# Probabilities and gate values handled two tiles at a time in an attention and gated feed-forward kernel

## The chip, the cores and the metric

The kernel runs on one core of one Trainium2 chip. Its time is the device time of one launch in microseconds, the median of three runs: 981.09 us (981.05 to 982.55). The core has a matrix engine (TensorE, PE in the profile), a vector engine (VectorE, DVE), an activation engine (ScalarE, ACT), a general engine (GpSimd, POOL) and a queue engine (SyncE, SP) that issues nearly all transfers. Each engine works through its own list of instructions strictly in the order in which the built program holds them; an instruction that waits for a semaphore holds back everything behind it in its list.

## The reference

```python
# attention: 4 batches x 8 heads, 768 positions, 64 channels
scores = scale * q @ k.T
mask = window of blocks | first/last block row and column | sampled blocks   # 24 x 24 blocks of 32
scores = where(mask, scores, -1e9); scores -= max(scores, axis=-1)
attn = exp(scores); attn = attn / (sum(attn, axis=-1) + 1e-9)
x = attn @ v                                   # (4*768) x 512 after the heads are joined
# feed-forward: 512 -> 2048 -> 512; weights come as float64
h = x @ w_in
g = h              where h >= 1
    0              where h <= -1
    (h + 1)**2 / 4 between
out = g @ w_out                                # float32
```

## The kernel before, in words

The 32 heads (4 batches of 8) are worked through one after the other. Beside the heads of batch b+1 runs the feed-forward part of batch b; the feed-forward part of the last batch runs alone at the end. Matrix products are made of two-part numbers: a value is split into a rounded high part and the rest, both in a format that TensorE streams at full speed (fp32r), and two or three products are summed in PSUM.

**A head** has 768 columns of queries, worked in two halves of 384 (`HALF`), and six key tiles of 128. First come 12 products for the row maxima (`max_mm`, L267), each followed by a maximum on VectorE (`max_red`, L272); their result goes into extra rows of the query operand, so that the scores come out already shifted. Then for each half and each key tile `c`: two score products (`scores`, L318 and L319), the exponential on ScalarE (`expo`, L323) from PSUM into a tile `pt`, the rounded high part on ScalarE (`p_hi`, in the helper at L196, tile `ph`), the rest on VectorE (`p_lo`, L331, tile `pl`), a running sum over key tiles on GpSimd (`p_sum`, L338, tile `acc`) and two products with the values (`values`, L350 and L351). At the end of a half, ScalarE copies one part of the result out of PSUM (`o_tmp`, L355, tile `otmp`), VectorE adds the other (`o_add`, L360), and `acc_sum` (L373) folds GpSimd's sum into `psum` on VectorE.

**Whole heads.** For the pairs of heads listed in `WHOLE` (before: 0 to 4, so heads 0 to 9) the probabilities are not split. The value product takes them as plain float32 (L348), and a column of ones beside the values gives the sums, so `p_hi`, `p_lo`, `p_sum`, `o_tmp`, `o_add` and `acc_sum` fall away.

**The feed-forward part** goes in 8 half batches of 384 rows, each over 16 blocks `fi` of 128 hidden units. For a block: 12 products into the PSUM tile `hp` (`l1`, L472 to L474), of which there is one buffer, so that the next block's products wait until this block's gate is finished; then the gate: `g_relu` and `g_sq` on ScalarE (L478, L481), `g_max` on VectorE (L484), which is the last to read `hp`; then the high part `gh` on ScalarE (`g_hi`, L196), the rest `gl` on VectorE (`g_lo`, L493), and 9 products of 512 columns (`l2`, L500 to L502; L500 and L501 read `gh`, L502 reads `gl`).

**Weights** come as float64 pairs of words. `convert` loads 512 KB into a buffer `raw`, makes float32 with four VectorE instructions of 512 columns (L169 to L174) and splits them (L196, L180). The first weight matrix is converted during the heads of batch 0, the second during the first half batch of the feed-forward part (beside heads 8 to 11), from where it goes to DRAM and is loaded again for later half batches.

**The order** is made in two steps. Every piece of work gets a due time (`at(t, fn)`), in units of one key tile; a head has 12 units (`PER`), a block `fi` has 3. Tables such as `P`, `PA` and `PW` hold the offsets (`'lag'` is the distance from the scores of a key tile to its value products, `'l2'` the one from `l1` to `l2`). The pieces are then issued by due time to a scheduler, which sets each engine's list by when operands and buffers come free in its own reckoning. The lists in the built program can thus differ from the due times. Pools with 2 or 3 buffers (`pp`, `mt`, `cv`) limit how far work can run ahead.

Of the kernel before, what the change touches and what calls it, by code (L numbers as in the profile page):

```python
# [21 lines left out]
HALF = 384  # L22
# [15 lines left out]
def body(ctx, tc, qk_t, v, sampled_blocks, moe_w_in, moe_w_out, ind, cm, negd, ident, fold, out):  # L38
# [7 lines left out]
    pp = pool("pp", 3)  # L46
# [40 lines left out]
    def consts():  # L87
# [69 lines left out]
    def convert(t, src, dst, done=None):  # L157
        st = {}

        def load():  # L160
            st["raw"] = cv.tile([128, 512, 2], I32, name="raw", bufs=3)
            Q_RAW.dma_start(out=st["raw"], in_=src.bitcast(I32).rearrange("p (c w) -> p c w", w=2))
# [35 lines left out]
    def head(i, n0, b, h, pst):  # L198
# [122 lines left out]
        def expo(c):  # L321
            p = st["p", c] = pp.tile([128, HALF], F32, name=("pt", "ph", "pl")[c % 3] if wide else "pt")
            nc.scalar.activation(out=p, in_=st.pop(("ps", c))[:, 0:HALF], func=AF.Exp, scale=SCALE)  # L323

        def p_hi(c):
            ph = st["ph", c] = pp.tile([128, HALF], F32R, name="ph")
            rounded(nc.vector if c in (PH1 if i < 2 * H else PH2) else nc.scalar, ph, st["p", c])

        def p_lo(c):
            pl = st["pl", c] = pp.tile([128, HALF], F32R, name="pl")  # L330
            (nc.gpsimd if i < 2 * H and c in PL1 else nc.vector).tensor_tensor(out=pl, in0=st["p", c], in1=f(st["ph", c]), op=ALU.subtract)  # L331

        def p_sum(hf, c):
            if c == 1:
                st["acc", hf] = ac.tile([128, HALF], F32, name="acc")
            if c:
                prev = st["p", 0] if c == 1 else st["acc", hf]
                nc.gpsimd.tensor_tensor(out=st["acc", hf], in0=prev, in1=st["p", c], op=ALU.add)  # L338
# [110 lines left out]
    def moe(t0, p, b, hf, first):  # L449
# [26 lines left out]
        def g_relu(fi):  # L476
            r = g["r", fi] = mt.tile([128, HALF], F32, name="r")
# [9 lines left out]
        def g_hi(fi):  # L487
            gh = g["gh", fi] = mt.tile([128, HALF], F32R, name="gh", bufs=3)
            rounded(nc.scalar, gh, g["r", fi])

        def g_lo(fi):
# [29 lines left out]
        for fi in range(NF):  # L521
# [14 lines left out]
            for t in range(3):  # L536
                at(u + G["l2"] * p + t * p * G["l3"], l2, fi, t)
# [106 lines left out]
```

## Time and profile before

| | |
|---|---|
| median of 3 runs | 981.09 us (981.05 to 982.55) |
| profiled execution, whole | 980.94 us |
| its span | 979.0 us |
| PE busy | 945.3 us, 97% |
| DVE busy | 736.8 us, 75% |
| ACT busy | 646.3 us, 66% |
| POOL busy | 251.5 us, 26% |
| mean granted TensorE clock | 0.995 |

Busy time is not throughput on TensorE: successive products overlap in the records. A 384-column product is drawn 0.34 us long, but the next one starts 0.17 to 0.18 us later. What matters is therefore the distance between the starts of neighbours in the list, and where it is longer than that. On VectorE and ScalarE neighbours overlap by about a tenth of a microsecond when the second does not need the first. A row of the timeline reads: start in us, length in us, engine, source line, operation, output tile <- input tiles, shape, count; at the end, in brackets, an idle time before it and what ended it.

### The profile page before, as it was taken

To read this page: it belongs to the slowest core of one execution; us is meant where nothing else is said; L and a number is where in the kernel's file an instruction comes from. 1 tells how busy PE (TensorE), PEld (TensorE's weight loads), DVE (VectorE), ACT (ScalarE), POOL (GpSimd) and SP (SyncE) were. 2 spreads that over 40 slices of the span, in tenths; PEclk is the share of its full clock that TensorE was granted. 3 is DMA by queue.
4 is the path that set the end of the run, shared out by engine and by line. 5 is a ranking of instruction groups with operands and counts; after the bars stand their busy time and mean duration, and the time that the engine had idled before them with its cause. 6 is when DMAs were issued, how large, how long until landed. Compare 5 with 4: busy or idle time off the path is not lost.

```text
span 979.0 us, 14671 instructions
## 1 busy us (share of the span) xinstructions
PE 945.3 (97%) x4746; PEld 833.3 (85%) x4746; DVE 736.8 (75%) x1390; ACT 646.3 (66%) x1326; POOL 251.5 (26%) x229
## 2 busy tenths in 40 slices
PE   5898999999899999999999999999999999999998
PEld 3676677888789999998999899999999999899997
DVE  5897988779998888988888888888788885422222
ACT  4686787677677676767677667776767676433433
POOL 1000000013334443433434343433434343000000
PEclk9899999999999999999999999999999999999999
DMA  6756766754364544545556453646445442433442
GB/s 193 227 155 183 200 201 214 259 173 140 129 205 144 146 148 136 178 135 154 158 154 189 118 153 120 198 138 176 137 143 178 126 114 89 154 129 129 161 129 97
DMA packets 56216, 154.44 MB, mean 158 GB/s; under 512 B 9612, under 2 KB 17952, under 8 KB 56140
## 3 DMA queue, kind: packets, MB, share of 16 engines
q1 hardware_dynamic: 56100, 153.48, 52.0%
q8 instruction: 38, 0.62, 0.3%
q14 instruction: 38, 0.31, 0.1%
q10 hardware_dynamic: 40, 0.03, 0.0%
HBM read 100.92 MB, written 14.81 MB: 118 GB/s over the span
## 4 chain that ended last, share of the span: by engine, by line
PE 88%; DVE 5%; ACT 3%; DMA 2%; issue 2%; SPq 0%; ACTq 0%; DVEq 0%
PE oa L500 8%; PE oa L502 8%; PE oa L501 8%; PE hp L472 8%; PE hp L474 8%; PE hp L473 8%; PE pa L267 7%; PE pa L318 5%; PE pa L319 5%; PE po L350 5%; PE po L348 5%; PE po L351 4%; PE oa L348 3%; DVE mc L272 1%; PE oa L318 1%
## 5 line engine op out<-in xcount | busy, mean ns | idle before, releaser
L338 POOL TENSOR_TENSOR acc<-acc,pt 128x384 f32<-128x384 f32 x176 | 202.2, 1149 | 226.2 <-ACT pt L323 190.3
L272 DVE TENSOR_REDUCE mc<-pa 128x1 f32<-128x384 f32 x384 | 202.8, 548 | 24.1 <-PE pa L267 21.0
L196 ACT CAST ph<-pt 128x384 fp32r<-128x384 f32 x264 | 135.7, 514 | 88.2 <-PE po L350 84.5
L331 DVE TENSOR_TENSOR pl<-pt,ph 128x384 fp32r<-128x384 f32 x264 | 166.3, 630 | 35.6 <-ACT ph L196 34.9
L323 ACT ACTIVATE pt<-pa 128x384 f32<-128x384 f32 x288 | 140.6, 489 | 50.8 <-PE pa L319 42.0
L472 PE MATMUL hp<-x,wi 128*128 128x384 f32 x448 | 155.0, 346 | 2.9 <-DVE r L484 2.9
L500 PE MATMUL oa<-w,gh 128*128 128x512 f32 x384 | 153.6, 400 | 0.3 <-ACT gh L196 0.3
L502 PE MATMUL oa<-w,gl 128*128 128x512 f32 x384 | 151.4, 394 | 0.0
L473 PE MATMUL hp<-x,wi 128*128 128x384 f32 x448 | 151.4, 338 | 0.0
L474 PE MATMUL hp<-x,wi 128*128 128x384 f32 x448 | 151.2, 338 | 0.0
L501 PE MATMUL oa<-w,gh 128*128 128x512 f32 x384 | 150.8, 393 | 0.0
L267 PE MATMUL pa<-KA,QA 88*128 88x384 f32 x384 | 138.8, 381 | 5.3 <-DMA QA<-qkh 3.0
L338 POOL TENSOR_TENSOR acc<-pt 128x384 f32<-128x384 f32 x44 | 45.8, 1040 | 349.4 <-ACT pt L323 349.4
L484 DVE SCALAR_TENSOR_TENSOR r<-r,hp 128x384 f32<-128x384 f32 x112 | 61.7, 551 | 74.0 <-ACT r L481 73.6
L493 DVE TENSOR_TENSOR gl<-r,gh 128x384 fp32r<-128x384 f32 x128 | 83.7, 654 | 23.4 <-ACT gh L196 22.9
L478 ACT ACTIVATE r<-hp,half_c 128x384 f32<-128x384 f32 x112 | 65.1, 582 | 53.4 <-PE hp L474 50.3
L318 PE MATMUL pa<-QA,KA 102*128 102x384 f32 x288 | 99.3, 345 | 0.8 <-ACT pt L323 0.4
L319 PE MATMUL pa<-QB,KB 128*128 128x384 f32 x288 | 97.9, 340 | 0.0
L267 PEld LDWEIGHTS pa<-KA,QA 88*128 88x128 f32 x384 | 73.2, 192 | 27.8 <-DVE mc L272 6.7
L350 PE MATMUL po<-ph,vn 128*128 128x384 f32 x264 | 91.5, 347 | 2.3 <-DVE xun L360 1.9
L472 PEld LDWEIGHTS hp<-x,wi 128*128 128x128 f32 x448 | 84.5, 189 | 8.6 <-DVE r L484 4.2
L351 PE MATMUL po<-pl,vn 128*128 128x384 f32 x264 | 88.6, 336 | 0.0
(100 smaller groups left out, 1634.1 us busy)
## 6 DMA issues: line engine op xcount, KB each, us to landing
w<-wo_dram SPq DMA_DIRECT2D x112, 512.0 KB
qk<-in_qk_t_dram SPq DMA_DIRECT2D x32, 384.0 KB
raw<-in_moe_w_in_dram SPq DMA_DIRECT2D x16, 512.0 KB
raw<-in_moe_w_out_dram SPq DMA_DIRECT2D x16, 512.0 KB
wo_dram<-w SPq DMA_DIRECT2D x16, 512.0 KB
lv<-in_v_dram SPq DMA_DIRECT2D x32, 192.0 KB
KA<-qkh SPq DMA_DIRECT2D x32, 192.0 KB
QA<-qkh SPq DMA_DIRECT2D x32, 192.0 KB
```

Source lines behind the costliest of these rows:

```text
L267: nc.tensor.matmul(out=pm[:, 0:HALF], lhsT=QAi[0:KM, t * 128:(t + 1) * 128], rhs=KAi[0:KM, kh * HALF:(kh + 1) * HALF], start=True, stop=True)
L272: nc.vector.reduce_max(out=st["mc"][:, t, kh:kh + 1], in_=st.pop(("pm", t, kh))[:, 0:HALF], axis=AX.X)
L318: nc.tensor.matmul(out=ps[:, 0:HALF], lhsT=KAi[0:KA, ks], rhs=QAi[0:KA, cs], start=True, stop=False)
L319: nc.tensor.matmul(out=ps[:, 0:HALF], lhsT=st["KB"][:, ks], rhs=st["QB"][:, cs], start=False, stop=True)
L331: (nc.gpsimd if i < 2 * H and c in PL1 else nc.vector).tensor_tensor(out=pl, in0=st["p", c], in1=f(st["ph", c]), op=ALU.subtract)
L338: nc.gpsimd.tensor_tensor(out=st["acc", hf], in0=prev, in1=st["p", c], op=ALU.add)
L472: nc.tensor.matmul(out=hv, lhsT=wi[:, j, 0, fs], rhs=x[:, 0], start=(j == 0), stop=False)
L473: nc.tensor.matmul(out=hv, lhsT=wi[:, j, 0, fs], rhs=x[:, 1], start=False, stop=False)
L474: nc.tensor.matmul(out=hv, lhsT=wi[:, j, 1, fs], rhs=x[:, 0], start=False, stop=(j == NP - 1))
L500: nc.tensor.matmul(out=o, lhsT=gh[:, ts], rhs=w[:, 0], start=(fi == 0), stop=False)
L501: nc.tensor.matmul(out=o, lhsT=gh[:, ts], rhs=w[:, 1], start=False, stop=False)
L502: nc.tensor.matmul(out=o, lhsT=gl[:, ts], rhs=w[:, 0], start=False, stop=(fi == NF - 1))
```

## The change

Five things change together.

- The exponentials of two neighbouring key tiles go into one tile `[128, 2, 384]`. `p_hi` and `p_lo` then work on a pair: one instruction of 768 columns in place of two of 384. `p_sum` adds pairs: per half two additions of 768 and one of 384 that folds the two halves of the sum, in place of five of 384.
- In the feed-forward part `g_relu`, `g_sq` and `g_max` stay per block, but `g_hi` and `g_lo` work on two blocks at once. Both blocks' `l2` products thus depend on the gate of the second one. Due times of `l2` move: by 0.6 of a block for even `fi`, by 0.2 for odd ones.
- The float64 buffers `raw` go from 3 to 2; `ph` and `pl` have 2 pairs in place of 3 single tiles, `pt` 3 pairs, `gh` and `gl` 2 pairs in place of 3 singles.
- `WHOLE` loses its last pair: heads 8 and 9, the first of batch 1, are now split like all later ones.
- The value products of split heads get the distance `LAG = 4.0` in place of 3.5, and the feed-forward parts start half a unit later (`DELAY`).

```diff
-        ef = f(cv.tile([128, 512, 2], I32, name="raw", bufs=3)...
+        ef = f(cv.tile([128, 512, 2], I32, name="raw", bufs=2)...
...
         def expo(c):
-            p = st["p", c] = pp.tile([128, HALF], F32, name=("pt", "ph", "pl")[c % 3] if wide else "pt")
+            cp, k = divmod(c, 2)
+            if k == 0:
+                st["pp", cp] = pp.tile([128, 2, HALF], F32, name=("pt", "ph", "pl")[cp] if wide else "pt",
+                                         bufs=2 if wide and cp else 3)
+            p = st["p", c] = st["pp", cp][:, k]
...
+        def p_hi(cp):
+            ph = st["php", cp] = pp.tile([128, 2, HALF], F32R, name="ph")
+            rounded(nc.scalar, ph, st["pp", cp])
+        def p_lo(cp):
+            pl = pp.tile([128, 2, HALF], F32R, name="pl")
+            nc.vector.tensor_tensor(out=pl, in0=st["pp", cp], in1=f(st["php", cp]), op=ALU.subtract)
+        def p_sum(hf, cp):
+            if cp == 0:
+                return
+            if cp == 1:
+                st["acc2", hf] = ac.tile([128, 2, HALF], F32, name="acc")
+            acc = st["acc2", hf]
+            nc.gpsimd.tensor_tensor(out=acc, in0=st["pp", 0] if cp == 1 else acc, in1=st["pp", cp], op=ALU.add)
+            if cp == 2:
+                nc.gpsimd.tensor_tensor(out=acc[:, 0], in0=acc[:, 0], in1=acc[:, 1], op=ALU.add)
...
-                if not whole:
-                    at(s + G["ph"], p_hi, c)
-                    at(s + G["pl"], p_lo, c)
-                    at(s + G["ps"], p_sum, hf, c)
-                at(s + G["lag"], values, hf, c)
+                if not whole and c % 2:
+                    at(s + G["ph"] - 0.5, p_hi, c // 2)
+                    at(s + G["pl"] - 0.5, p_lo, c // 2)
+                    at(s + G["ps"], p_sum, hf, c // 2)
+                at(s + (G["lag"] if whole else LAG), values, hf, c)
...
+        def g_hi(fp):
+            gh = g["ghp", fp] = mt.tile([128, 2, HALF], F32R, name="gh")
+            rounded(nc.scalar, gh, g["rr", fp])
+        def g_lo(fp):
+            gl = mt.tile([128, 2, HALF], F32R, name="gl")
+            nc.vector.tensor_tensor(out=gl, in0=g["rr", fp], in1=f(g["ghp", fp]), op=ALU.subtract)
...
-            at(m + G["gh"], g_hi, fi)
-            at(m + G["gl"], g_lo, fi)
+            if fi % 2:
+                at(m + G["gh"], g_hi, fi // 2)
+                at(m + G["gl"] + 0.1, g_lo, fi // 2)
+            w = u + G["l2"] * p + (0.6 * p if fi % 2 == 0 else 0.2 * p)
             for t in range(3):
-                at(u + G["l2"] * p + t * p * G["l3"], l2, fi, t)
+                at(w + t * p * G["l3"], l2, fi, t)
...
-WHOLE = (0, 1, 2, 3, 4)
+WHOLE = (0, 1, 2, 3)
+LAG = 4.0
-DELAY = 3.672
+DELAY = 4.172
```

Three places in the engines' lists show what the scheduler makes of it. They lie in the steady part, at head 22 and at the feed-forward blocks that stand 57th and 58th of the 128 (counted from 0; called 57 and 58 below, an odd and an even one).

The first place is ScalarE's list around the gate of block 57: the exponential (`pt`), the gate's two steps (`r`), the copy `otmp` and the rounding `gh`. Before:

```order
L478 ACTIVATE r<-hp,half_c 128x384
L323 ACTIVATE pt<-pa 128x384
L481 ACTIVATE r<-r 128x384
L196 CAST ph<-pt 128x384
L355 COPY otmp<-po 64x384
L196 CAST gh<-r 128x384
```

And now:

```order
L327 ACTIVATE pt<-pa 128x384
L490 ACTIVATE r<-hp,half_c 128x384
L493 ACTIVATE r<-r 128x384
L365 COPY otmp<-po 64x384
L327 ACTIVATE pt<-pa 128x384 x2
L196 CAST gh<-r 128x768
```

Between the square (the last `r<-r`) and `gh` stood `ph` and `otmp`; now `otmp` and two exponentials stand there, and `gh` is 768 wide.

The second place is TensorE's list after the last `l1` product of block 57 (`hp<-x,wi`), up to the products that read its `gh` and `gl`. Before, 41 rows lie between the first and the last row shown:

```order
L474 MATMUL hp<-x,wi 128x384
L267 MATMUL pa<-KA_116,QA_114 128x384
L318 MATMUL pa<-QA_113,KA_115 128x384
L319 MATMUL pa<-QB,KB 128x384
...
L500 MATMUL oa_6170<-w,gh 128x512
L501 MATMUL oa_6170<-w,gh 128x512
L502 MATMUL oa_6170<-w,gl 128x512
```

And now, up to the products of block 56, which reads the first half of the same `gh`:

```order
L484 MATMUL hp<-x,wi 128x384
L267 MATMUL pa<-KA_116,QA_114 128x384 x2
L360 MATMUL po<-ph,vn 128x384
L361 MATMUL po<-pl,vn 128x384
L318 MATMUL pa<-QA_113,KA_115 128x384
L319 MATMUL pa<-QB,KB 128x384
...
L514 MATMUL oa_5783<-w,gh 128x512
L515 MATMUL oa_5783<-w,gh 128x512
L293 MATMUL pa<-idr,mr 6x128
L516 MATMUL oa_5783<-w,gl 128x512
```

Between the last `l1` product and the first reader of `gh` there are now 17 products of 384 columns: two for maxima, four for values, four for scores and seven of the next block's `l1` (in the lines left out). Before, the nine products that read block 56's gate stood in between as well. At the same place after block 59 there are 14, after blocks 61 and 63 there are 15 and 14 and one small product.

The third place is VectorE's list at the end of head 22, with `g_max` of block 58 (`r<-r,hp`), which frees `hp` for block 59. Before:

```order
L331 TENSOR_TENSOR pl<-pt,ph 128x384
L484 SCALAR_TENSOR_TENSOR r<-r,hp 128x384
L331 TENSOR_TENSOR pl<-pt,ph 128x384
L373 TENSOR_REDUCE psum<-acc 128x12
L493 TENSOR_TENSOR gl<-r,gh 128x384
```

And now:

```order
L506 TENSOR_TENSOR gl<-r,gh 128x768
L336 TENSOR_TENSOR pl<-pt,ph 128x768
L298 TENSOR_TENSOR QA_114<-pa,nd 6x768
L336 TENSOR_TENSOR pl<-pt,ph 128x768
L383 TENSOR_REDUCE psum<-acc 128x12
L496 SCALAR_TENSOR_TENSOR r<-r,hp 128x384
```

`g_max` stood ahead of the head's last `pl` and of `psum`, which waits for GpSimd's sum; now it stands behind both.

More of the change, by code (lines that the diff above doesn't have):

```diff
@@ L45, in body @@
     vp = pool("vp", 2)
-    pp = pool("pp", 3)
+    pp = pool("pp", 2)
     ac = pool("ac", 2)
@@ L160, in load @@
         def load():
-            st["raw"] = cv.tile([128, 512, 2], I32, name="raw", bufs=3)
+            st["raw"] = cv.tile([128, 512, 2], I32, name="raw", bufs=2)
             Q_RAW.dma_start(out=st["raw"], in_=src.bitcast(I32).rearrange("p (c w) -> p c w", w=2))
@@ L321, in expo @@
         def expo(c):
-            p = st["p", c] = pp.tile([128, HALF], F32, name=("pt", "ph", "pl")[c % 3] if wide else "pt")
[L323 to L338, printed above, removed]
+            cp, k = divmod(c, 2)
[3 more added lines that the diff above has]
+            p = st["p", c] = st["pp", cp][:, k]
+            nc.scalar.activation(out=p, in_=st.pop(("ps", c))[:, 0:HALF], func=AF.Exp, scale=SCALE)
+        def p_hi(cp):
+            ph = st["php", cp] = pp.tile([128, 2, HALF], F32R, name="ph")
+            rounded(nc.scalar, ph, st["pp", cp])
+            st["ph", 2 * cp], st["ph", 2 * cp + 1] = ph[:, 0], ph[:, 1]
+        def p_lo(cp):
+            pl = pp.tile([128, 2, HALF], F32R, name="pl")
+            nc.vector.tensor_tensor(out=pl, in0=st["pp", cp], in1=f(st["php", cp]), op=ALU.subtract)
+            st["pl", 2 * cp], st["pl", 2 * cp + 1] = pl[:, 0], pl[:, 1]
+        def p_sum(hf, cp):
[7 more added lines that the diff above has]
+                nc.gpsimd.tensor_tensor(out=acc[:, 0], in0=acc[:, 0], in1=acc[:, 1], op=ALU.add)
+                st["acc", hf] = acc[:, 0]
         def values(hf, c):
@@ L416, in head @@
                 at(s + G["ex"], expo, c)
-                if not whole:
-                    at(s + G["ph"], p_hi, c)
-                    at(s + G["pl"], p_lo, c)
-                    at(s + G["ps"], p_sum, hf, c)
-                at(s + G["lag"], values, hf, c)
+                if not whole and c % 2:
[3 more added lines that the diff above has]
+                at(s + (G["lag"] if whole else LAG), values, hf, c)
                 s += 1
-            u = s - 1 + G["lag"]
+            u = s - 1 + (G["lag"] if whole else LAG)
             if whole:
@@ L485, in g_max @@
                                            op0=ALU.min, op1=ALU.max)
[L487 to L491, printed above, removed]
-            gl = g["gl", fi] = mt.tile([128, HALF], F32R, name="gl", bufs=3)
-            (nc.gpsimd if first and fi % 4 in GL1 else nc.vector).tensor_tensor(out=gl, in0=g["r", fi], in1=f(g["gh", fi]), op=ALU.subtract)
+        def g_hi(fp):
+            gh = g["ghp", fp] = mt.tile([128, 2, HALF], F32R, name="gh")
+            rounded(nc.scalar, gh, g["rr", fp])
+            g["gh", 2 * fp], g["gh", 2 * fp + 1] = gh[:, 0], gh[:, 1]
+        def g_lo(fp):
+            gl = mt.tile([128, 2, HALF], F32R, name="gl")
+            nc.vector.tensor_tensor(out=gl, in0=g["rr", fp], in1=f(g["ghp", fp]), op=ALU.subtract)
+            g["gl", 2 * fp], g["gl", 2 * fp + 1] = gl[:, 0], gl[:, 1]
         def l2(fi, t):
```

12 lines of the change are left out of this document (7 added, 5 removed).

## The prediction

> **What bounds the kernel now.** I read the page first, then the busy time by stretch, then the idle time in front of the feed-forward products, and last the order in time of single instructions.
>
> ```profile
> PE 945.3 (97%) x4746; PEld 833.3 (85%) x4746; DVE 736.8 (75%) x1390; ACT 646.3 (66%) x1326; POOL 251.5 (26%) x229
> ...
> 195.80:293.70 97.90, 90.64 (x458) 78.16 (x457) 91.41 (x164) 70.31 (x148) 30.66 (x26) 1.00 0.50 162
> 293.70:832.20 538.50, 536.05 (x2821) 493.83 (x2820) 444.76 (x832) 382.81 (x800) 216.66 (x194) 1.00 0.50 147
> 832.20:979.00 146.80, 142.53 (x716) 128.06 (x714) 42.52 (x78) 59.60 (x112) 0.65 (x1) 1.00 0.39 133
> ...
> L500 PE MATMUL oa<-w,gh 128*128 128x512 f32 x384 | 153.6, 400 | 0.3 <-ACT gh L196 0.3
> L502 PE MATMUL oa<-w,gl 128*128 128x512 f32 x384 | 151.4, 394 | 0.0
> L472 PE MATMUL hp<-x,wi 128*128 128x384 f32 x448 | 155.0, 346 | 2.9 <-DVE r L484 2.9
> ```
>
> The three stretches (columns: length, then busy time of PE, weight load, DVE, ACT, POOL) are the heads 8 to 11 with the weight conversion, the heads 12 to 31, and the last batch's feed-forward part. In the second and third TensorE has no holes; its products stand in line. In the first VectorE is busy 91.41 of 97.90 us: there it is the bound, or nearly. The last three rows say the same from the other side: of all idle time in front of the feed-forward products only 0.3 us is a wait for `gh`, none for `gl`, and 2.9 us for the gate that frees `hp`. So over 685 us nothing gains time but work taken off TensorE, and everything that makes TensorE wait costs its full length.
>
> Why it does not wait today shows at one block (the odd block 57 of the order rows above):
>
> ```profile
> 573.65 0.34 PE L473 MATMUL hp<-x,wi 128*128 128x384 f32 x1
> 573.83 0.34 PE L474 MATMUL hp<-x,wi 128*128 128x384 f32 x1
> 581.30 0.39 PE L500 MATMUL oa<-w,gh 128*128 128x512 f32 x1
> 581.53 0.40 PE L501 MATMUL oa<-w,gh 128*128 128x512 f32 x1
> 574.21 0.58 ACT L478 ACTIVATE r<-hp,half_c 128x384 f32<-128x384 f32 x1 [0.32 <-PE hp L474]
> 574.80 0.49 ACT L323 ACTIVATE pt<-pa 128x384 f32<-128x384 f32 x1
> 575.18 0.52 ACT L481 ACTIVATE r<-r 128x384 f32<-128x384 f32 x1
> 576.38 0.48 ACT L355 COPY otmp<-po 64x384 f32<-64x384 f32 x1
> 576.76 0.51 ACT L196 CAST gh<-r 128x384 fp32r<-128x384 f32 x1
> 577.29 0.49 ACT L323 ACTIVATE pt<-pa 128x384 f32<-128x384 f32 x1
> 577.93 1.33 POOL L338 TENSOR_TENSOR acc<-acc,pt 128x384 f32<-128x384 f32 x1 [1.48 <-ACT pt L323]
> 578.29 1.38 DVE L493 TENSOR_TENSOR gl<-r,gh 128x384 fp32r<-128x384 f32 x1
> ```
>
> The last `l1` product starts at 573.83, `gh` is finished at 577.27 (576.76 + 0.51), `gl` at 579.67, and the first product that reads them starts at 581.30. Some 7.3 us of other products lie in between, against 5.7 us that the slower of the two takes. The rows also give TensorE's spacing: 0.175 us for 384 columns, 0.23 for 512.
>
> **The change, part by part.**
>
> *Heads 8 and 9 split.* A whole product and its split successor:
>
> ```profile
> 210.14 0.81 PE L348 MATMUL po<-pt,vn 128*128 128x384 f32 x2
> 210.96 0.34 PE L473 MATMUL hp<-x,wi 128*128 128x384 f32 x1
> 579.96 0.34 PE L350 MATMUL po<-ph,vn 128*128 128x384 f32 x1
> 580.14 0.34 PE L351 MATMUL po<-pl,vn 128*128 128x384 f32 x1
> 580.31 0.22 PE L293 MATMUL pa<-idr,mr 128*6 128x128 f32 x1
> ```
>
> From 210.14 to 210.96 lie the whole product and one L472 of 0.175 us, so it holds TensorE for 0.645 us; the two split ones take 0.35 (579.96 to 580.31). 24 of them: 24 x 0.295 = 7.1 us less on TensorE. But they lie in the stretch that VectorE bounds, and VectorE gets work.
>
> ```profile
> L228 DVE TENSOR_TENSOR qk<-qk,qkh 128x768 f32<-128x768 f32 x32 | 34.6, 1081 | 1.3 <-ACT qkh L196 1.2
> 579.68 0.54 DVE L331 TENSOR_TENSOR pl<-pt,ph 128x384 fp32r<-128x384 f32 x1
> 580.15 0.94 DVE L228 TENSOR_TENSOR qk<-qk,qkh 128x768 f32<-128x768 f32 x1
> 573.10 0.57 DVE L373 TRANSPOSE_TENSOR_REDUCE psum<-acc 128x12 f32<-128x384 f32 x1
> 569.85 0.83 ACT L196 CAST qkh<-qk 128x768 fp32r<-128x768 f32 x1 [0.63 <-DMA qk<-in_qk_t_dram]
> 570.59 0.48 ACT L323 ACTIVATE pt<-pa 128x384 f32<-128x384 f32 x1
> ```
>
> The trace has 768-column instructions of the same kinds: 0.94 us on VectorE when nothing hinders it (its mean of 1081 ns does hold hindrances), 0.83 on ScalarE. Neighbours are 0.47 apart on VectorE for 384 columns (579.68 to 580.15), that is 0.08 of overlap, so a 768 one takes 0.86 of the engine in place of 2 x 0.47 = 0.94: pairing saves 0.08 per pair, not half. On ScalarE it is 0.74 (569.85 to 570.59) in place of two times 0.41 (0.51 less the tenth of overlap), again 0.08. Heads 8 and 9 add on VectorE 12 pairs x 0.86 = 10.3 us, and four times an `o_add` (0.47) and an `acc_sum` (0.57 less the overlap) = 3.8; pairing gives back 20 x 0.08 = 1.6 there. 91.4 + 12.5 = 103.9 us no longer fit into 97.9. If VectorE is packed full, the stretch takes 6 us longer; if TensorE's saving comes through whole, 7 us less; if VectorE keeps the 93% it has now and the waits below come on top, some 21 more. I take **+6**, since VectorE stands at 93% already.
>
> *The gate by pairs of blocks.* This is the large term. Both blocks' products now wait for the second block's gate, and the order rows show 17, 14, 15 and 14 products of 384 columns between its last `l1` product and the first reader of `gh`, in four pairs that repeat every two heads. At 0.175 us that is 2.97, 2.45, 2.68 and 2.51 us of cover, where 7.3 stood. What the chain needs can be read at the end of the run, where nothing else runs:
>
> ```profile
> 969.97 0.34 PE L474 MATMUL pa<-x,wi 128*128 128x384 f32 x1
> 970.34 0.58 ACT L478 ACTIVATE r<-pa,half_c 128x384 f32<-128x384 f32 x1 [1.90 <-PE pa L474]
> 970.95 0.53 ACT L481 ACTIVATE r<-r 128x384 f32<-128x384 f32 x1
> 971.51 0.55 DVE L484 SCALAR_TENSOR_TENSOR r<-r,pa 128x384 f32<-128x384 f32 x1 [2.48 <-ACT r L481]
> 972.10 0.51 ACT L196 CAST gh<-r 128x384 fp32r<-128x384 f32 x1 [0.62 <-DVE r L484]
> 972.66 0.50 PE L500 MATMUL oa<-w,gh 128*128 128x512 f32 x1 [0.28 <-ACT gh L196]
> ```
>
> From the end of the last `l1` product's turn (969.97 + 0.175 = 970.14) it is 0.20 to the gate's first step, 0.81 to the square, 2.52 to the first reader. With `gh` at 0.83 in place of 0.51 that is 2.84 bare. In the steady part ScalarE's list now has `otmp` and two exponentials between square and `gh`. With neighbours a tenth apart in overlap (574.80 to 575.18 for an exponential of 0.49, 576.38 to 576.76 for `otmp`) the square holds the engine to 1.24, `otmp` to 1.62, the exponentials to 2.00 and 2.38, `gh` ends at 3.21 and TensorE can go on at 3.26. The gate's VectorE step is done by 1.92 and does not count. In two of the four pairs a copy of `vn` (0.51) stands in between too, which moves all by 0.29. Waits for `gh`: 0.29, 1.1, 0.58, 1.04.
>
> Then `gl`, 0.94 long, which TensorE wants 0.5 to 1.2 us after `gh` (two `gh` products and what stands between): at 3.49, 3.43, 3.55 and 3.69. Undisturbed it is there at 4.2 or 4.5, which makes the whole wait of a pair 0.7, 1.1, 0.65 and 1.05, on average 0.88. But it is not undisturbed. In the fence of block 57, `gl` took 1.38 us where 0.55 is its usual length: a GpSimd addition ran from 577.93 to 579.26, and `gl` ended 0.41 behind it. So VectorE's subtraction stands still until GpSimd's addition is through, and then needs its length less 0.14. Now GpSimd's first pair addition starts 0.1 to 0.15 us behind the first of the two exponentials (577.78 to 577.93 above), at 2.2 us on the same scale, a microsecond ahead of `gl`, and it is 768 wide.
>
> ```profile
> L338 POOL TENSOR_TENSOR acc<-pt 128x384 f32<-128x384 f32 x44 | 45.8, 1040 | 349.4 <-ACT pt L323 349.4
> L90 POOL MEMSET QA<- 64x768 f32 x2 | 1.4, 732 | 0.3 <-POOLq L624 0.3
> L91 POOL MEMSET vn<- 128x384 f32 x1 | 0.4, 427 | 0.1
> ```
>
> No 768 addition is in the trace. It takes at least the 1.02 of a 384 one and at most twice that; the memsets (427 ns for 384, 732 for 768) leave 0.12 fixed, which makes 0.12 + 2 x 0.90 = 1.92. I take 1.9, as the row nearest in kind scales that way. The addition then ends at 4.1 (4.4 with `vn`), `gl` at 4.9 (5.2), and the waits become 1.46, 1.8, 1.4, 1.55: on average 1.55 a pair. Heads 12 to 31 have 40 pairs: **+62**, with 35 if GpSimd does not hinder, and 13 for the bare chain (0, 0.4, 0.16 and 0.33 for `gh`; about 0.32 with `gl`). What ScalarE and VectorE have less to do meanwhile is worth nothing, since they wait for TensorE.
>
> The Trainium skill, SBUF — State Buffer, section "SBUF: two separate sides", says that a VectorE instruction with two SBUF inputs and a GpSimd one that reads SBUF take a port pair as an exclusive lock for the whole instruction. By that rule the 62 holds and not the 35; the row of 1.38 agrees.
>
> *The sum by pairs.* `acc_sum` now follows two additions of 1.9 and 1.02 behind the last exponential, and at every second head stands ahead of the `g_max` that frees `hp` (the third place of the order). Behind the last score product lie 0.2 + 0.49 + 0.1 + 1.9 + 1.02 + 0.57 + 0.55 = 4.8 us until `hp` is free; TensorE's list has 11 products of 384 and 9 of 512 columns there, 11 x 0.175 + 9 x 0.23 = 4.0. So 0.8 us at every second head, 10 times: **+8**. Where the last `pl` too stands behind GpSimd, it is up to 1.3 a head: 26. With a shorter addition: 0.
>
> *The last part.* After `l1` of an odd block 16 products lie ahead of `gh`'s reader, 2.73 us against 2.84 + 0.05, with `gl` 0.16 short: 15 pairs, 2.4 us. The last pair cannot be covered: before, 9 products of the last block but one (9 x 0.23 = 2.1) fill most of the 2.52, then none fill the 2.84; 2.4 us more. Together **+5**, between 2 and 6.
>
> *Two raw buffers, the wider distances.* Conversions are due 5.75 units apart, 12 us; 512 KB at the mean 158 GB/s of the page take 3.3. With two buffers a load starts one conversion earlier than its use, and hides. If VectorE is late the load is late by as much; 0, with 0 to 4. `LAG` and `DELAY` shift work on a full TensorE: 0.
>
> Sum: 979.0 + 6 + 62 + 8 + 5 = 1060 us of span. The profiled execution took 980.94, 1.9 beyond its span and 0.15 below the median, so **1062 us**.
>
> **The rivals.**
>
> *GpSimd does not hinder* (its wide addition is short, or `gl` gets ahead of it). For: GpSimd stands at 26%. Against: the row of 1.38. 979 + 6 + 35 + 8 + 5 + 2 = 1035.
>
> *Only the bare chain counts*, because the exponentials are through before the square. Against: their scores are in TensorE's list behind the last `l1` product. 979 + 0 + 13 + 0 + 5 + 2 = 999.
>
> *Faster: the saving on TensorE comes through.* The pairs' gates are finished in time, heads 8 and 9 shorten TensorE's list by 7.1 us, and VectorE, relieved of 0.08 a pair, does not hold the stretch back: 979 - 7 + 2 + 2 = 976. It decides if the wait is below 7.1 / 40 = 0.18 us a pair. For: TensorE is the bound and its list gets shorter. Against: even the bare chain is longer than three of the four covers.
>
> *Slower still*: the transfers that wait for a weight buffer sit in SP's one queue, and when TensorE is late those behind them are too; over 1096.
>
> **How the numbers follow.** The forecast, 1062, has 52%; GpSimd not hindering, 1035, 25%; the bare chain, about 999, 8%; faster, 976, 8%; no change 2%; slower still 5%. The low end is that second case with the first stretch at its best and no wait for sums, 979 - 7 + 35 + 0 + 2 + 2 = 1011, drawn to 1005 for part of the third; what it leaves out there is the rest of the third, no change and faster. The high end is 979 + 21 + 62 + 26 + 6 + 2 = 1096. Under 0.2% (2 us) no difference can be told here. Faster 8%, same 2%, slower 90%.
>
> **What would show it.** Right: idle time in front of L514 with the release by ACT `gh`, and of L516 with DVE `gl`, together near 60 us; PE busy falling well below 97% between the conversion and the last part; the row of `gl` 768 wide with a mean well above 0.94; GpSimd's 768 row near 1.9; a short wait of L482 for `g_max`; the last part 5 us longer. Wrong: `gl` at 0.94 on average (then 1035), GpSimd's wide addition near 1.0, or L514 and L516 with no idle time and the first stretch shorter (then 976). If the waits are there but TensorE's spacing closes up elsewhere, my premise that the list has no holes to give is wrong.

## The result and the profile after

The changed kernel takes 1124.83 us (median of 6 runs, 1123.4 to 1132.7) against 981.07 us before (6 runs): 1.148 times as long, 95% interval 1.144 to 1.151, or 144 us. The forecast was 1062, its range 1005 to 1096. The profiled execution took 1124.95 us, its span is 1123.1.

In the kernel before, the chain of work that ended last stood almost wholly on TensorE:

```profile
PE 88%; DVE 5%; ACT 3%; DMA 2%; issue 2%; SPq 0%; ACTq 0%; DVEq 0%
```

In the changed kernel, the head of the page and the groups that answer to those of the prediction (columns: busy time in us and mean of one in ns; then idle time in front and what ended it):

```profile
PE 998.5 (89%) x4750; PEld 830.2 (74%) x4750; DVE 795.2 (71%) x1218; ACT 619.3 (55%) x1138; POOL 259.1 (23%) x153
...
PE 49%; DVE 28%; ACT 11%; issue 5%; DMA 4%; POOL 4%; SPq 0%; POOLq 0%; ACTq 0%; DVEq 0%
...
L336 DVE TENSOR_TENSOR pl<-pt,ph 128x768 fp32r<-128x768 f32 x144 | 178.6, 1240 | 62.6 <-ACT ph L196 32.1
L345 POOL TENSOR_TENSOR acc<-pt 128x768 f32<-128x768 f32 x48 | 89.3, 1861 | 514.5 <-ACT pt L327 514.5
L345 POOL TENSOR_TENSOR acc<-acc,pt 128x768 f32<-128x768 f32 x48 | 92.1, 1918 | 185.8 <-ACT pt L327 185.8
L347 POOL TENSOR_TENSOR acc<-acc 128x384 f32<-128x384 f32 x48 | 74.2, 1546 | 3.8
L482 PE MATMUL hp<-x,wi 128*128 128x384 f32 x448 | 160.5, 358 | 39.4 <-DVE r L496 39.3
L516 PE MATMUL oa<-w,gl 128*128 128x512 f32 x384 | 152.3, 409 | 22.4 <-DVE gl L506 22.3
L514 PE MATMUL oa<-w,gh 128*128 128x512 f32 x384 | 157.5, 410 | 4.2 <-ACT gh L196 3.6
L267 PE MATMUL pa<-KA,QA 88*128 88x384 f32 x384 | 134.8, 388 | 28.3 <-DVE mc L272 17.6
...
L506 DVE TENSOR_TENSOR gl<-r,gh 128x768 fp32r<-128x768 f32 x64 | 75.3, 1176 | 20.8 <-ACT gh L196 20.8
```

TensorE fell from 97% to 89%, and the chain that ended last now leads over VectorE for 28% of the span (5% before). The two wide additions take 1.86 and 1.92 us on average (forecast 1.9) and `gl` 1.18 (0.94 when no addition runs as it starts). But the longest wait is not that for `gl`: it is that for `hp`, 39.3 us, and 17.6 more are waits for a bank that a maximum (`mc`) still reads.

From here on the span is cut where the turn of the last `l1` product of feed-forward blocks 0, 16 and 96 ends (0.175 us behind its start). The second piece, 16 blocks long, is the conversion stretch with about heads 8 to 11 (it begins earlier than the prediction's, which was cut at 195.8); the third, 80 blocks, holds about heads 12 to 31; the fourth is the last batch's feed-forward part. Busy time by stretch, before (columns: length, then busy time of PE, weight load, DVE, ACT, POOL, then granted TensorE clock, DMA share and GB/s):

```profile
163.00:284.80 121.80, 114.54 (x567) 97.36 (x567) 109.05 (x197) 85.95 (x176) 28.27 (x24) 1.00 0.56 182
284.80:841.00 556.20, 553.75 (x2913) 509.92 (x2913) 458.28 (x858) 393.50 (x821) 219.70 (x196) 1.00 0.51 148
841.00:979.00 138.00, 133.73 (x670) 120.17 (x668) 37.30 (x67) 56.14 (x105) 0.00 (x0) 1.00 0.40 134
```

and after:

```profile
163.70:308.80 145.10, 124.99 (x578) 105.66 (x578) 136.72 (x212) 90.64 (x165) 42.02 (x23) 0.92 0.49 160
308.80:978.00 669.20, 593.59 (x2905) 502.75 (x2904) 493.00 (x698) 366.25 (x663) 208.25 (x119) 1.00 0.42 122
978.00:1123.10 145.10, 138.84 (x679) 119.76 (x677) 35.77 (x52) 52.67 (x90) 0.00 (x0) 1.00 0.42 130
```

The 144 us are 23.3 in the conversion stretch, 113.0 in heads 12 to 31, 7.1 in the last part and 0.7 ahead of them. In heads 12 to 31 VectorE runs 160 instructions fewer and is yet busy 35 us longer.

How `hp` comes late shows at one place of the changed kernel, seen in time (start, length; GpSimd, ScalarE, VectorE, TensorE):

```profile
562.40 1.85 POOL L345 TENSOR_TENSOR acc<-acc,pt 128x768 f32<-128x768 f32 x1 [4.40 <-ACT pt L327]
564.32 1.60 POOL L347 TENSOR_TENSOR acc<-acc 128x384 f32<-128x384 f32 x1
...
563.63 0.53 ACT L493 ACTIVATE r<-r 128x384 f32<-128x384 f32 x1
...
563.16 1.90 DVE L336 TENSOR_TENSOR pl<-pt,ph 128x768 fp32r<-128x768 f32 x1 [1.90 <-PE po L360]
564.98 1.36 DVE L412 TENSOR_TENSOR xun<-xun,den 128x384 f32<-128x384 f32 x1
566.27 0.54 DVE L496 SCALAR_TENSOR_TENSOR r<-r,hp 128x384 f32<-128x384 f32 x1
...
565.40 0.34 PE L319 MATMUL pa<-QB,KB 128*128 128x384 f32 x1
566.86 0.44 PE L482 MATMUL hp<-x,wi 128*128 128x384 f32 x1 [1.11 <-DVE r L496]
```

`g_max` (L496) could have begun at 564.16, when the square was done. It began at 566.27, because two instructions stood ahead of it. `pl` started 0.76 us into GpSimd's wide addition and ended 0.81 after it (its own length is 0.95, the mean in a kernel without GpSimd's additions, h1 below). GpSimd's last addition then started at once, but ended only at 565.92, 0.86 after `pl`; and the product `xun` behind `pl`, 0.55 long by itself, ended 0.42 after that. The two engines held each other by turns, and TensorE stood 1.11 us at the end of the line. The row sums (`psum`) do not even stand ahead of `g_max` here.

### The profile page after: what moved, and what is told of

Same layout as the page of the kernel before. It is cut to its first block, busy times and chain, and to the rows that moved or that the text cites. A ratio compares the mean times of both kernels' runs of the same rounds, so it can differ in the third digit from the quotient of the medians.

```text
span 1123.1 us, 13671 instructions
## 1 busy us (share of the span) xinstructions
PE 998.5 (89%) x4750; PEld 830.2 (74%) x4750; DVE 795.2 (71%) x1218; ACT 619.3 (55%) x1138; POOL 259.1 (23%) x153
## 4 chain that ended last, share of the span: by engine, by line
PE 49%; DVE 28%; ACT 11%; issue 5%; DMA 4%; POOL 4%; SPq 0%; POOLq 0%; ACTq 0%; DVEq 0%
PE oa L516 7%; PE oa L514 5%; DVE pl L336 5%; PE oa L515 5%; DVE gl L506 5%; PE hp L484 4%; DVE mc L272 4%; PE hp L482 4%; PE hp L483 4%; PE pa L267 4%; ACT pt L327 3%; DVE r L496 2%; PE pa L318 2%; PE pa L319 2%; PE po L360 2%
## 5 line engine op out<-in xcount | busy, mean ns | idle before, releaser
L336 DVE TENSOR_TENSOR pl<-pt,ph 128x768 fp32r<-128x768 f32 x144 | 178.6, 1240 | 62.6 <-ACT ph L196 32.1
L345 POOL TENSOR_TENSOR acc<-pt 128x768 f32<-128x768 f32 x48 | 89.3, 1861 | 514.5 <-ACT pt L327 514.5
L482 PE MATMUL hp<-x,wi 128*128 128x384 f32 x448 | 160.5, 358 | 39.4 <-DVE r L496 39.3
L267 PE MATMUL pa<-KA,QA 88*128 88x384 f32 x384 | 134.8, 388 | 28.3 <-DVE mc L272 17.6
L484 PE MATMUL hp<-x,wi 128*128 128x384 f32 x448 | 153.0, 341 | 0.0
L483 PE MATMUL hp<-x,wi 128*128 128x384 f32 x448 | 152.7, 341 | 0.0
L345 POOL TENSOR_TENSOR acc<-acc,pt 128x768 f32<-128x768 f32 x48 | 92.1, 1918 | 185.8 <-ACT pt L327 185.8
L196 ACT CAST ph<-pt 128x768 fp32r<-128x768 f32 x144 | 120.5, 837 | 4.4 <-PE po L360 1.4
L267 PEld LDWEIGHTS pa<-KA,QA 88*128 88x128 f32 x384 | 73.4, 194 | 61.0 <-DVE mc L272 31.9
L516 PEld LDWEIGHTS oa<-w,gl 128*128 128x128 f32 x384 | 70.6, 189 | 49.6 <-DVE gl L506 37.2
L360 PE MATMUL po<-ph,vn 128*128 128x384 f32 x288 | 99.5, 345 | 3.0 <-DVE xun L370 2.6
L361 PE MATMUL po<-pl,vn 128*128 128x384 f32 x288 | 98.4, 342 | 1.2 <-DVE pl L336 1.2
L514 PEld LDWEIGHTS oa<-w,gh 128*128 128x128 f32 x384 | 73.1, 190 | 23.5 <-ACT gh L196 17.4
L506 DVE TENSOR_TENSOR gl<-r,gh 128x768 fp32r<-128x768 f32 x64 | 75.3, 1176 | 20.8 <-ACT gh L196 20.8
```

The source lines that it names most:

```text
L267: nc.tensor.matmul(out=pm[:, 0:HALF], lhsT=QAi[0:KM, t * 128:(t + 1) * 128], rhs=KAi[0:KM, kh * HALF:(kh + 1) * HALF], start=True, stop=True)
L336: nc.vector.tensor_tensor(out=pl, in0=st["pp", cp], in1=f(st["php", cp]), op=ALU.subtract)
L345: nc.gpsimd.tensor_tensor(out=acc, in0=st["pp", 0] if cp == 1 else acc, in1=st["pp", cp], op=ALU.add)
L482: nc.tensor.matmul(out=hv, lhsT=wi[:, j, 0, fs], rhs=x[:, 0], start=(j == 0), stop=False)
L483: nc.tensor.matmul(out=hv, lhsT=wi[:, j, 0, fs], rhs=x[:, 1], start=False, stop=False)
L484: nc.tensor.matmul(out=hv, lhsT=wi[:, j, 1, fs], rhs=x[:, 0], start=False, stop=(j == NP - 1))
```

## The experiments

Twelve kernels. The lengths of the last three pieces come from each one's profiled execution, which in a1 and c2 took 6.0 and 4.2 us longer than the median and in h2 3.2 less; a difference of pieces with one of these is good to several us. "Wide" means sums by 768 columns, "narrow" by 384; "pairs" is the gate by pairs of blocks. e2 and i1 have all else as before; the others have the pair tiles of probabilities and the later due times of the changed kernel.

| kernel | sums | gate | heads 8, 9 | time | ratio to before (95%) | heads 8–11 | heads 12–31 | last |
|---|---|---|---|---|---|---|---|---|
| before | narrow | blocks | whole | 981.1 | | 121.8 | 556.2 | 138.0 |
| changed | wide | pairs | split | 1124.8 | 1.144–1.151 | 145.1 | 669.2 | 145.1 |
| a1 | wide | blocks | split | 1054.7 | 1.070–1.082 | 142.8 | 610.3 | 137.8 |
| c1 | narrow | pairs | split | 1074.0 | 1.092–1.100 | 139.4 | 620.0 | 145.0 |
| c2 | narrow | blocks | split | 1001.5 | 1.018–1.024 | 134.8 | 561.4 | 137.8 |
| c3 | narrow | blocks | whole | 984.4 | 1.001–1.005 | 122.3 | 560.4 | 138.0 |
| b1 | wide | blocks | whole | 1034.9 | 1.052–1.057 | 122.4 | 608.8 | 138.9 |
| d1 | none | pairs | split | 1029.2 | 1.044–1.054 | 123.7 | 593.6 | 146.6 |
| d2 | wide, unread | pairs | split | 1095.0 | 1.112–1.121 | 142.4 | 639.2 | 146.4 |
| h1 | none | blocks | split | 982.0 | 0.999–1.003 | 118.5 | 558.0 | 137.8 |
| h2 | wide, unread | blocks | split | 1023.6 | 1.040–1.050 | 136.7 | 579.6 | 137.8 |
| e2 | narrow | blocks | split | 994.8 | 1.012–1.017 | 134.8 | 553.8 | 137.7 |
| i1 | narrow | blocks | whole, 10, 11 too | 980.5 | 0.997–1.002 | 119.0 | 558.6 | 138.1 |
| g1 | wide | pairs, `l2` later | split | 1065.6 | 1.082–1.087 | 137.2 | 618.8 | 141.5 |

### Is it the sums? (d1, d2)

d1 leaves GpSimd's additions out; d2 makes them, but nobody reads them:

```diff
 def p_sum(hf, cp):                    # d1
-    ...                               # three additions
+    if cp == 2:
+        st["acc", hf] = st["pp", cp][:, 0]
...
                 nc.gpsimd.tensor_tensor(out=acc[:, 0], in0=acc[:, 0], in1=acc[:, 1], op=ALU.add)
-                st["acc", hf] = acc[:, 0]          # d2
+                st["acc", hf] = st["pp", cp][:, 0]
```

> The changed kernel with GpSimd's additions of the probabilities left out (each denominator is reduced from one key tile's probabilities instead, so the sums over the key tiles are not computed); every other instruction stays. The changed kernel takes 1124.8 us. Theory: GpSimd's wide additions hold VectorE, and through it hp and the score banks. Without them the waits of a gate pair fall from 1.55 to 0.88 us (40 pairs, -27), the hp waits beyond the pairs' own vanish (-32), so do those for the banks of the maxima (-17), and the conversion stretch gives back about 8: near 1040 us. Rival (the sums' dependency alone: the row sums stand ahead of g_max in VectorE's list and wait for GpSimd's last addition): the same as the kernel with the sums computed but unread. Rival (GpSimd has no part in it): 1115 to 1125.

> The changed kernel with GpSimd's additions still made, but read by nobody: each denominator is reduced from one key tile's probabilities, as in the kernel without additions, so the sums are not used. It differs from that one by the additions alone. Theory (GpSimd's presence holds VectorE): gains only the wait of the row sums for the last addition, some 10 us, 1110 to 1118. Rival (the dependency): gains all of the hp wait beyond the pairs' own, 1085 to 1095, and equals the kernel without additions.

Measured: d1 1029.2, d2 1095.0. The lists of TensorE and VectorE are the same in both, so 66 us are what the additions cost by running alone, with no result of theirs in use. A further 30 (1124.8 - 1095.0) hang on the row sums waiting for them, and on the place in VectorE's list that the scheduler gives them for it. I had put that second share at 10; it is three times that, and d1 came out 11 below its 1040. Neither theory is the whole: both causes are real. The wait and the place in the list were not taken apart.

What the place in the list is worth shows at the block of the place at 562 us, here in d2:

```profile
549.46 1.85 POOL L345 TENSOR_TENSOR acc<-acc,pt 128x768 f32<-128x768 f32 x1 [4.38 <-ACT pt L327]
551.38 1.61 POOL L347 TENSOR_TENSOR acc<-acc 128x384 f32<-128x384 f32 x1
...
550.21 1.91 DVE L336 TENSOR_TENSOR pl<-pt,ph 128x768 fp32r<-128x768 f32 x1 [1.52 <-PE po L360]
552.04 0.54 DVE L496 SCALAR_TENSOR_TENSOR r<-r,hp 128x384 f32<-128x384 f32 x1
552.51 0.90 DVE L412 TENSOR_TENSOR xun<-xun,den 128x384 f32<-128x384 f32 x1
...
552.47 0.34 PE L319 MATMUL pa<-QB,KB 128*128 128x384 f32 x1
552.64 0.44 PE L482 MATMUL hp<-x,wi 128*128 128x384 f32 x1
```

`pl` is held as long as in the changed kernel, but `g_max` follows directly, takes its usual 0.54 us beside GpSimd's last addition, and TensorE goes on without a gap. In heads 12 to 31 TensorE loses 26.2 us in front of the first `l1` product after an even block in the changed kernel and 0.2 in d2 (worked out as under g1 below). Of the 26.2, 16.0 lie at the 13 places where `psum` stands directly ahead of `g_max`, and 10.2 at eight others, where `pl` and `xun` stand ahead of it as at 562 us.

### Are the gate's pairs a cost of their own? (a1, c1, c2)

a1 takes the gate back to single blocks, c1 the sums back to five additions of 384, c2 both:

```diff
-            if fi % 2:                                   # a1
-                at(m + G["gh"], g_hi, fi // 2)
-                at(m + G["gl"] + 0.1, g_lo, fi // 2)
+            at(m + G["gh"], g_hi, fi)
+            at(m + G["gl"], g_lo, fi)
...
+            for c in (2 * cp, 2 * cp + 1):               # c1
+                if c:
+                    prev = st["p", 0] if c == 1 else st["acc", hf]
+                    nc.gpsimd.tensor_tensor(out=st["acc", hf], in0=prev, in1=st["p", c], op=ALU.add)
```

> The changed kernel with the gate's casts and subtractions, and the due times of the products that read them, block by block as before; probabilities, sums, buffers and heads 8 and 9 stay changed. Theory (pairs of blocks leave too little cover): the waits for gh and gl, the hp wait that follows from the same chain and the last part's go: 61 + 6, about 1058 us. Rival (VectorE is late anyway, and TensorE would wait elsewhere for as long): over 1095. Rival (the pair gate causes nearly all, GpSimd's hold included): under 1010.

> The changed kernel with GpSimd's sum of a head in five additions of 384 columns, as before, in place of two of 768 and one of 384; TensorE's and ScalarE's lists stay. The same columns are added in all, 5.1 us a head against about 5.4. Theory (one addition holds VectorE for its own length): a hold is at most 1.0 in place of 1.9, gl waits fall by about 0.5 us a pair (-20) and the hp and bank waits by half (-24): near 1080 us. Rival (the total of GpSimd's time counts, not its pieces): 1115 to 1130.

> The changed kernel with both: the gate block by block (1054.7 us alone) and the sums in five additions of 384 columns (1074.0 alone). What stays of the change: exponentials in pair tiles, casts and subtractions of the probabilities 768 wide, heads 8 and 9 split, two raw buffers, later due times. Theory (gate pairs and wide sums are all that costs in heads 12 to 31): these give back 111 us there and 7 in the last part, the conversion stretch keeps what the split of heads 8 and 9 costs it: 985 to 1000 us. Rival (the wide subtractions of the probabilities cost as well, since GpSimd holds them longer than two narrow ones): 1010 to 1035.

Measured: 1054.7, 1074.0, 1001.5. The theories had 1058, near 1080 and 985 to 1000. The two causes add up in the total. Pairs cost 70.1 us with wide sums (1124.8 - 1054.7) and 72.5 with narrow ones (1074.0 - 1001.5); wide sums cost 50.8 with pairs and 53.2 without. In heads 12 to 31 the pairs cost 58.9 and 58.6, the wide sums 49.2 and 48.9. Place by place they do not add up. With wide sums, 39 of the pairs' 59 us in heads 12 to 31 are lost in front of the readers of `gh` and `gl`; with narrow ones 20, and 24 in front of `l1` and 15 in front of the maxima's products (worked out as under g1 below).

That c1 regains 51 us although GpSimd is busy longer than in the changed kernel (284 us against 259) shows that it is not the total of the additions that counts. It does not show that it is the length of one alone: VectorE's list differs too. In heads 12 to 31 of c1 `psum` never stands directly ahead of `g_max`, and the 26.2 us lost after even blocks are 2.2.

### Split by cause with the gate by blocks (h1, h2)

The edits of d1 and d2, each made in a1.

> The changed kernel with the gate block by block and GpSimd's additions left out (denominators from one key tile's probabilities, so the sums are not computed). With the additions this kernel takes 1054.7 us. Theory: all of its 41 us of hp waits and 15 us of waits for the maxima's banks in heads 12 to 31 come from GpSimd, and most of the 21 us of the conversion stretch: near 985 us. Rival (the 768 wide subtractions jam VectorE by themselves): over 1005.

> The same kernel with GpSimd's wide additions made but read by nobody (denominators as in the kernel without additions). The two differ by the additions alone. Theory (half by half): the dependency of the row sums, which stand ahead of g_max in VectorE's list at 30 of 48 places, is worth 30 us as under the pair gate (1054.7 to about 1025), and the additions' mere presence some 40. Rival (with the gate by blocks nothing waits for gl, so presence costs little): 990 to 1000. Rival (presence is all): 1050.

Measured: 982.0 and 1023.6, as the theories had it (985 and 1025). Without additions the kernel with everything else of the change but the gate's pairs is as fast as before (which makes the additions of the heads that it splits). The presence of the additions costs 41.6 us, the dependency 31.1 more. Since the two kernels have the same lists, the same rows can be laid side by side. VectorE's groups in h1 (no additions):

```profile
L272 DVE TENSOR_REDUCE mc<-pa 128x1 f32<-128x384 f32 x384 | 201.1, 550 | 30.4 <-PE pa L267 26.9
L336 DVE TENSOR_TENSOR pl<-pt,ph 128x768 fp32r<-128x768 f32 x144 | 136.3, 946 | 59.3 <-ACT ph L196 45.4 <-PE po L353 13.1
L496 DVE TENSOR_TENSOR gl<-r,gh 128x384 fp32r<-128x384 f32 x128 | 71.1, 555 | 37.7 <-ACT gh L196 37.1
L376 DVE TRANSPOSE_TENSOR_REDUCE psum<-pt 128x12 f32<-128x384 f32 x48 | 27.3, 568 | 0.1
...
L169 DVE TENSOR_SCALAR cva<-cva 128x512 f32<-128x512 f32 x32 | 13.4, 417 | 6.2 <-ACT cva L168 6.1
...
L276 DVE TENSOR_TENSOR mr<-mc 128x6 fp32r<-128x6 f32 x32 | 4.9, 153 | 0.2
```

and in h2 (additions made, unread):

```profile
L272 DVE TENSOR_REDUCE mc<-pa 128x1 f32<-128x384 f32 x384 | 197.9, 545 | 17.8 <-PE pa L267 15.7
L336 DVE TENSOR_TENSOR pl<-pt,ph 128x768 fp32r<-128x768 f32 x144 | 174.2, 1209 | 19.3 <-ACT ph L196 18.9
L503 DVE TENSOR_TENSOR gl<-r,gh 128x384 fp32r<-128x384 f32 x128 | 98.5, 769 | 36.0 <-ACT gh L196 35.7
...
L383 DVE TRANSPOSE_TENSOR_REDUCE psum<-pt 128x12 f32<-128x384 f32 x48 | 26.9, 560 | 0.1
...
L276 DVE TENSOR_TENSOR mr<-mc 128x6 fp32r<-128x6 f32 x32 | 20.0, 625 | 0.2
...
L169 DVE TENSOR_SCALAR cva<-cva 128x512 f32<-128x512 f32 x32 | 17.2, 536 | 4.5 <-ACT cva L168 4.4
```

`pl` goes from 946 to 1209 ns, `gl` from 555 to 769, `mr`, six columns wide, from 153 to 625, and L169, a copy-like instruction with one input in SBUF, from 417 to 536. The maxima (`mc`), which read PSUM, and the row sums (`psum`), a reduction with one input, do not change. The additions also read `pt`, and so could keep its buffers from ScalarE; that is not the cost: ScalarE's `pt` waits 1.8 us in all for GpSimd in h2, 1.1 in d2, and no such wait is listed for the changed kernel. The Trainium skill, SBUF — State Buffer, section "Who interferes with whom", draws that line: VectorE contends with GpSimd where it has two SBUF inputs or a copy-like instruction in its two-port mode, not in a reduction. These rows agree; whether L169 runs in that mode no row tells.

### Heads 8 and 9, and what is left (b1, e2, c3, i1)

b1 and c3 are a1 and c2 with heads 8 and 9 whole again (b1 also with three raw buffers); e2 and i1 are the kernel before with `WHOLE` of four and of six pairs of heads.

> The kernel with the gate block by block, heads 0 to 9 whole as before, three raw buffers as before; changed are the probabilities by pairs, the wide sums and the later due times. Against the one with the gate by blocks (1054.7 us) it differs in heads 8 and 9 and the raw buffer. Theory (the conversion stretch, 21 us longer there, is long because VectorE is held by the wide additions of the split heads; with only heads 10 and 11 split it loses half): 1040 to 1046 us. Rival (the split of heads 8 and 9 is the whole cause there): 1034. Rival (the split is nothing, it is heads 10 and 11 and the conversions' own subtractions): 1052 to 1058.

> The kernel before with one edit: heads 8 and 9 split too, as in the change. Theory of the prediction (VectorE bounds that stretch): 6 us longer, 987. Rival (TensorE's saving of 7.1 us comes through there when GpSimd's additions are narrow): 973 to 976. In between, no change.

> The kernel with narrow sums and the gate by blocks (1001.5 us), heads 8 and 9 whole again as before. What is left of the change: pair tiles of exponentials, 768 wide casts and subtractions of the probabilities, two raw buffers, later due times. Theory (the parts add up; the split costs 12.6 us): 986 to 990, 5 to 8 above the kernel before. Rival (these leftovers cost nothing, the 7 us belong to the split): 981.

> The kernel before with heads 10 and 11 whole too, the opposite of the change's split: TensorE gets 24 x 0.295 = 7.1 us more, VectorE 12.5 us less in the conversion stretch, of whose 121.8 us TensorE stands still for 17.4. Theory (VectorE bounds the stretch): the standing still goes and the products stay, 981 + 7 - 12 = 976, or no change if part of the 17.4 has other causes. Rival (there TensorE bounds already): 988.

Measured: b1 1034.9, e2 994.8, c3 984.4, i1 980.5. b1 hit its rival: with heads 8 and 9 whole the conversion stretch is back at 122.4 us with wide sums, and c3 has 122.3 with narrow ones. e2 lies above its theory (987) and its rival: the split alone costs 13.0 us in this stretch with narrow sums; with all of the change it grows by 23.3. With the split and no additions at all it is 3.3 shorter than before (h1: 118.5). h1 also lacks the additions of heads 10 and 11, and no run has heads 8 and 9 whole without additions, so what the split alone costs without them is not shown. c3 lies between its theory and its rival and leaves 3.3 us (0.1 to 0.5%) for the pair tiles, the two raw buffers and the later due times together. i1, the opposite edit, is no different from before. The conversion stretch by the same columns as above, in h1:

```profile
166.50:284.90 118.40, 113.20 (x578) 99.42 (x578) 113.28 (x217) 89.17 (x171) 0.00 (x0) 0.99 0.62 197
```

and in e2:

```profile
166.10:300.90 134.80, 119.37 (x577) 102.74 (x576) 129.98 (x230) 90.79 (x191) 46.44 (x39) 0.95 0.51 166
```

VectorE's work for the split heads is in both; busy for 113 us in one, for 130 in the other. The granted clock differs as well: 1.00 before, 0.99 in h1, 0.95 in e2, 0.92 in the changed kernel. It does not set the length: c2's stretch is as long as e2's at 0.97, and d2's 142.4 us at 0.96 are as long as a1's 142.8 at 0.92. Some us of it can still be the clock's; no run takes that apart. The first piece, ahead of these, holds the first half of head 8 (in the split kernels with wide sums, three of its additions); it is 164 to 170 us long in the profiles with heads 8 and 9 split and 162 to 164 in those with them whole; that part of the split's price was not followed further.

### More products between gate and reader (g1)

```diff
-            w = u + G["l2"] * p + (0.6 * p if fi % 2 == 0 else 0.2 * p)
+            w = u + G["l2"] * p + (1.2 * p if fi % 2 == 0 else 0.8 * p)
```

> The changed kernel with the products that read gh and gl moved 0.6 of a block period further back in TensorE's list, so that some 14 more products lie between an odd block's last l1 product and the first reader. Theory: the waits in front of those readers (41 us of TensorE's time in heads 12 to 31) go, the waits for hp (52 us) stay, and the last part is as long: near 1085 us. Rival (the wait only moves, to hp or the banks): over 1110. Rival (with the waits gone the lists close up and VectorE falls less behind): under 1060.

Measured: 1065.6, between the theory and the second rival. Of the changed kernel's time this regains 59 us. Worked out over all products of heads 12 to 31, as the distance between the starts of neighbours beyond the usual one (0.175 us after 384 columns, 0.23 after 512), TensorE's lost time in front of the readers of `gh` and `gl` falls from 41 to 5 us, and that in front of `l1`, which I had left as it was, from 52 to 27. Most of this second gain is at one kind of place: in front of the first `l1` product after an odd block 16.5 us were lost and 0.9 are left. That product waits for the odd block's `g_max`, which in the changed kernel mostly ends 1.9 to 2.2 us behind the block's last `l1` product; only 7 to 10 products of 384 columns, 1.2 to 1.75 us, stand between the two (3.1 to 4.3 us of products in the kernel before, 2.6 to 3.1 in g1). In return 17 us are lost in front of score products (8 in the changed kernel).

None of these kernels beats the one before.

## Why the prediction was wrong

The direction and the largest term were right, the size was not: +81 was forecast, +144 came. What failed above all is the term for the sums, 8 forecast and 49 measured, and after it the conversion stretch, 6 and 23. One path of single steps through the runs is +3.3 (c3), +17.1 for the split (c2), +72.5 for the gate's pairs (c1), +50.8 for the wide sums, in all 143.7.

- **The gate by pairs, +62 and +5: right in size, only in part in place.** Measured 59 in heads 12 to 31 and 7.1 in the last part. The case in which GpSimd does not hinder was put at 35; d1 against h1, without additions, gives 593.6 - 558.0 = 35.6. So the additions do lift the price about as forecast, and in the steady part `gl` ended 5.2 to 5.7 us behind the last `l1` product (4.9 to 5.2 in the forecast), 4.4 to 4.7 without additions. That the width of the addition is the reason is not shown: with narrow sums the pairs cost 58.6 as well, though `gl` then ended at 4.7 at the median and not at 5.4. And the forecast put all 62 in front of the readers of `gh` and `gl`; 39 are lost there, and 16.5 in front of the next block's first `l1` product. For that wait it had nothing: "The gate's VectorE step is done by 1.92 and does not count." But seven of the 17 products that it counts as cover are `l1` products, which wait for that very step, and only ten stand ahead of them. What TensorE loses there it need not wait again for `gl`, which is later still; that the total came out so near is in part luck.
- **The sum by pairs, +8 with 26 as its upper bound: the step that failed.** Measured 49 in heads 12 to 31. It is two terms, and both were mis-sized. The dependency was 8 and is 30 (669.2 - 639.2 = 30.0; 610.3 - 579.6 = 30.7). The forecast had ten places at 0.8 us each. The trace has 13 places with `psum` directly ahead of `g_max`; 11 of them make TensorE wait, 1.45 us at the median. I took the last addition as 1.02 us from the row of the kernel before; in the changed kernel `pl` slips in ahead of it and it takes 1.55 (74.2 us for 48). The other 10.2 us lie at eight places like the one at 562 us, 1.28 us each at the median, where a held `pl` and a held `xun` and not `psum` stand ahead of `g_max`. The presence was priced only as an upper bound, one held `pl` a head, and taken as nothing; it is 18 beyond what narrow sums cost (579.6 - 561.4), in about equal parts in front of the maxima's products and of `l1`. The place at 562 us shows why one hold is too few in both terms: the next instruction with two SBUF inputs is held by the next addition, and whatever stands behind both, `g_max` or the maxima that need no GpSimd at all, is late by the sum. Hence the 17.6 us in front of L267, a wait the forecast did not have.
- **The conversion stretch, +6 out of -7 to +21: wrong in its reason.** Measured +23.3. I read "VectorE busy 91.41 of 97.90 us" as its own work, to which 12.5 us would be added. h1 runs that added work in a shorter stretch than before. The busy time held time in which VectorE's instructions were stopped by GpSimd; splitting heads 8 and 9 brings GpSimd into two more heads, and that was the cost: 13 with narrow additions and the gate by blocks (c2, e2), 21 to 23 with wide ones (a1 and the changed kernel), 15 and 21 where nobody reads them (h2, d2). The rival in which TensorE's 7 us come through was right in that VectorE's own work fits. Whether the 7 us would come through in a kernel without additions is open: h1 is 3.3 shorter than before in this stretch, 3.5 longer ahead of it, and as long in all.
- **Raw buffers, `LAG` and `DELAY`, 0: nearly right.** Together with the pairs of probabilities they come to the 3.3 us of c3. In h1 `pl` takes 946 ns for 768 columns, the 0.94 of the forecast, and what it saves VectorE buys nothing that shows, as the forecast said.
- **The rivals.** "GpSimd does not hinder" and "bare chain" fall with d1 and d2. "Slower still" came true in its number, but not by its mechanism: DMA has 4% of the chain (2% before) and no part of it in heads 12 to 31, and from 164 us on the engines' listed waits for transfers come to 2.7 us.
- **The range.** Its upper end added 21, 62, 26 and 6; the second held, and the first and the last came out a little above (23.3 and 7.1). With 49 in place of 26 it would have reached 1119. Heads 12 to 31 hold 5 more that no term had: c2's 561.4 against 556.2, of which c3, with 560.4, has most.

## What to carry to other kernels

Halving the number of instructions on an engine that is not the bound saved nothing here, and a wider instruction can make its readers wait longer: before pairing, count the products that lie between the last producer and the first reader, and leave out those that themselves wait for the same step. Where GpSimd and VectorE both read SBUF, price a longer GpSimd instruction by everything that stands behind the held VectorE instruction in its list, not by the held one alone. A busy VectorE next to a running GpSimd is not proof of work: leave GpSimd's additions out once and see what its busy time is then.

## What the runs showed of the hardware

The hold goes both ways and by turns: GpSimd's last addition of 384 columns takes a median 1.60 us at the 39 of 48 places where `pl` got in ahead of it, where the same width takes 1.00 at its shortest in the kernel before. The wide addition is 1.85 us at the median, 1.83 at its shortest. A VectorE instruction of six columns (`mr`, 153 ns) took 625 ns on average next to wide additions, and 808 in the changed kernel: 14 that started while an addition ran took 1.65 us on average, the others 0.15. `pl` likewise took 1.83 us on average at the 48 places where it started beside an addition, 0.95 at the other 96. Reductions and instructions with one input in PSUM kept their time to within 10 ns between h1 and h2. So, on average, did L172 and L174, which have two SBUF inputs: in h2 none of them started while an addition ran; in the changed kernel one of each did and took 1.85 and 2.35 us, where 0.69 is the most in h1.
